# Weight-sum units, token sums, token loads and the gate row at other steps of a fused attention and SwiGLU block

## The chip, the cores and the metric

The kernel runs on one core of one Trainium2 chip. The metric is the device time of one execution in microseconds (us), a median over runs. Times inside an execution come from one profiled run of a kernel; they are counted from the first instruction.

The experiments ran in four batches on three chips, each batch with its own runs of the kernel before on the same chip.

## The reference, cut to what matters

```python
mod = silu(c) @ w_mod                      # six rows: sa, ca, ga, sb, cb, gb
h = layernorm(x) * (1 + ca) + sa           # x: 2048 tokens x 1024
q = h @ wq                                 # 32 heads of 128
o = softmax(q @ k.T / sqrt(128)) @ v       # the last 512 keys of 4 cached k/v heads
x = x + ga * (o @ wo)
h = layernorm(x) * (1 + cb) + sb
x = x + gb * ((silu(h @ w_gate) * (h @ w_up)) @ w_down)      # 3584 wide
```

## The kernel before

The tokens go through attention in two halves: attention 1, projection 1 (with `wo`), attention 2, projection 2. Then gate/up and the down projection follow, once per half. An attention is 64 steps; a step works on one head and 512 tokens. All large products but scores and values use a scheme with seven products instead of eight, which needs sums of weight blocks. These sums are made once, by GpSimd, as 58 **units**: 16 of `wo`, 28 of `w_gate` and `w_up`, 14 of `w_down`. A unit loads 512 KB into a staging slot of SBUF, does eight additions in place and writes 512 KB of sums to DRAM. Later loads fetch them.

A helper tracks which instruction last wrote or read a piece of SBUF and puts the waits in front of an instruction. All SBUF in question is one arena, where different tensors take the same bytes at different times. Each engine has a queue of its own, filled in the order in which the instructions are emitted. What stands behind a waiting instruction of ScalarE waits with it; the profile below shows this, with 21.77 us.

```python
OFF_ST = [131 * KB, 138 * KB]              # the two staging slots of units
OFF_U = 144 * KB                           # the slot in gate/up

def unit_step(ring):                       # emits one unit: load, sums, write
    k = un["c"]
    if k >= len(units):
        return
    while un["l"] - k < max(len(ring) - 1, 1):
        unit_ahead(ring)                   # load this one, if it is not loaded yet
    un["c"] += 1
    for n, _ in enumerate(unit_sums(k)):   # 4 pairs of additions on GpSimd
        if n == 1 and un["l"] - k < len(ring):
            unit_ahead(ring)               # with two slots: load the next one
    unit_write(k)

def unit_tick(i):                          # in an attention, NI = 64 steps
    if i % 5 in (0, 2):
        unit_step(OFF_ST if i % NI < NI - 14 else OFF_ST[1:])

def tick0(i):                              # attention 1; attention 2 likewise
    if i < 20 or i % 4 == 2:
        run_x()                            # a part of a gate row (ga or gb), if there is one
    wq_tick(0, i)
    if 6 <= i < NI - 8:
        unit_tick(i)

def o_units(sc, idx, j):                   # in a projection: 7 product groups
    if j == 1 and idx > 1 and (sc or idx % 2 == 0):
        unit_step(OFF_ST[1:])
```

The end of an attention also loads the weights of the projection. `start_o` names their places; the second part of the first set (131 KB on) and the second set (133 to 145 KB) lie over both staging slots:

```python
places = [[(OFF_WQ, 14), (131 * KB, 2)], [(133 * KB, 12), (OFF_E, 4)]] + ...

for i in range(lo, hi + 2):                # attend(): one step
    ...
    scores(i - 1)                          # TensorE, then exp on ScalarE
    pv(i - 2)                              # TensorE: needs that exp
    ...
    if i == hi - 6:
        start_o(sc)                        # first part of the first set
    if i == hi - 1:
        wo0[sc][0](0, (1,))                # these loads are issued by ScalarE
        wo0[sc][0](1)
```

`h_sums` makes four sums of token blocks on VectorE, each over 128 x 2048 elements, in a row. `stats_task` takes LayerNorm statistics of tokens in the background; its last two instructions per tile are on GpSimd.

The softmax here doesn't subtract the row's maximum and nothing guards it: scores larger than these inputs give would overflow.

## Time and profile before

| | before |
|---|---|
| median, range | 1223.62 us, 1223.05 to 1225.3 (4 runs) |
| span of the profiled run | 1223.2 us |
| TensorE busy | 1154.5 us, 94% |

Every product group needs the TensorE, so at 94% busy the kernel is bound by it, and what can still be won is its idle time, about 69 us. The page of the profile shows this; the first line gives busy times, the second a group of instructions (busy us and mean ns of one, then the idle time just before them and what ended most of it):

```profile
PE 1154.5 (94%) x7002; PEld 591.4 (48%) x7087; DVE 735.3 (60%) x1297; ACT 527.9 (43%) x735; POOL 452.8 (37%) x655
...
L273 PE MATMUL ps<-arena 128*128 128x512 f16 (+2 forms) x6697 | 1146.7, 332 | 64.5 <-ACT arena L784 31.0
```

The waits of the TensorE (total us, number, longest) blame the exponentials of line 784 first:

```profile
PE ps L273 <- ACT arena L784: 31.0, 5, 18.3
PE ps L273 <- DVE arena L806: 10.7, 2, 5.8
PE ps L273 <- issue: 4.1, 2, 3.9
```

The timeline of the end of attention 2 shows what stands behind this (start, duration, engine, line, operation; in brackets the idle time before it and its releaser). ACTq and POOL L950/L927 are DMA issues: L950 a unit's write, L927 a unit's load.

```profile
587.99 0.65 POOL L950 DMA_DIRECT2D wgu_sum<-arena  x1 [0.30 <-POOL arena L882]
...
589.53 0.80 POOL L927 DMA_DIRECT2D arena<-in_B_w_down_dram  x1
593.25 12.15 ACTq L1144 DMA_DIRECT2D arena<-in_A_wo_dram  x3
...
601.15 0.57 POOL L950 DMA_DIRECT2D wd_sum<-arena  x1 [0.30 <-POOL arena L943]
...
605.45 2.14 ACT L784 ACTIVATE arena<-ps 128x1024 bf16<-128x1024 f32 x2 [21.77 <-POOL rstd L419]
...
607.64 17.56 PE L273 MATMUL ps<-arena 128*128 128x129 bf16 x81 [18.34 <-ACT arena L784]
```

ScalarE stands still from 583.68 to 605.45, the 21.77 us in the bracket, with three loads in front of the exponentials in its queue. The line of 593.25 merges the three. Their places lie over the slots, so each waits until its slot is free. The exponentials start at 605.45, and the TensorE goes on at 607.64 after 18.34 us. The bracket of line 605.45 names an instruction of GpSimd that merely ran last before. The end of attention 1 looks the same, with 10.95 us (its line of 255.41 merges a load at 255.41 and two at 269.43):

```profile
255.41 15.25 ACTq L1144 DMA_DIRECT2D arena<-in_A_wo_dram  x3
...
266.40 0.57 POOL L950 DMA_DIRECT2D wgu_sum<-arena  x1 [0.30 <-POOL arena L882]
270.72 2.14 ACT L784 ACTIVATE arena<-ps 128x1024 bf16<-128x1024 f32 x2 [14.38 <-issue]
...
272.91 1.91 PE L273 MATMUL ps<-arena 128*128 128x129 bf16 x16 [10.95 <-ACT arena L784]
```

The windows (busy us and instructions of TensorE, weight loads, VectorE, ScalarE, GpSimd; then granted clock, DMA share, GB/s) show that a long wait costs more than itself. For 4 us after it the TensorE has half its clock:

```profile
607.60:611.70 4.10, 4.06 (x22) 2.62 (x23) 0.87 (x2) 0.00 (x0) 0.00 (x0) 0.50 0.98 319
611.70:616.00 4.30, 4.25 (x20) 1.89 (x20) 2.87 (x4) 0.00 (x0) 0.00 (x0) 0.99 0.15 30
```

Third, GpSimd's own timeline shows how the units run: the first in projection 1 (299.20), the first in attention 2 (373.81), and some in its middle:

```profile
299.20 0.94 POOL L927 DMA_DIRECT2D arena<-in_B_w_gate_dram  x1 [32.23 <-PE ps L273]
...
373.81 0.93 POOL L927 DMA_DIRECT2D arena<-in_B_w_up_dram  x1 [22.14 <-ACT tmp L817]
...
426.91 0.59 POOL L950 DMA_DIRECT2D wgu_sum<-arena  x1 [0.30 <-POOL arena L882]
...
433.79 0.94 POOL L927 DMA_DIRECT2D arena<-in_B_w_up_dram  x1 [3.05 <-DMA wgu_sum<-arena]
...
438.90 0.59 POOL L950 DMA_DIRECT2D wgu_sum<-arena  x1 [0.30 <-POOL arena L882]
```

These two writes are 12 us apart; over attention 2 it is (601.15 - 373.81) / 22 = 10.3 us per unit. The waits between them are for DMA transfers of the units themselves, never for another engine. New units are offered every 2.5 steps of 3.5 us, so every 8.75 us. GpSimd therefore falls behind all through attention 2.

Last, the four token sums of attention 1 delay what VectorE must do for the TensorE:

```profile
117.78 1.68 DVE L830 TENSOR_TENSOR arena<-arena 128x2048 f16<-128x2048 f16 x1
...
120.34 1.91 PE L273 MATMUL ps<-arena 128*128 128x129 bf16 x16 [4.96 <-DVE arena L806]
```

### The profile page before, as it was taken

To read this page: it belongs to the slowest core of one execution; us is meant where nothing else is said; L and a number is where in the kernel's file an instruction comes from. 1 tells how busy PE (TensorE), PEld (TensorE's weight loads), DVE (VectorE), ACT (ScalarE), POOL (GpSimd) and SP (SyncE) were. 2 spreads that over 40 slices of the span, in tenths; PEclk is the share of its full clock that TensorE was granted. 3 is DMA by queue.
4 is the path that set the end of the run, shared out by engine and by line. 5 is a ranking of instruction groups with operands and counts; after the bars stand their busy time and mean duration, and the time that the engine had idled before them with its cause. 6 is when DMAs were issued, how large, how long until landed. Compare 5 with 4: busy or idle time off the path is not lost.

```text
span 1223.2 us, 18300 instructions
## 1 busy us (share of the span) xinstructions
PE 1154.5 (94%) x7002; PEld 591.4 (48%) x7087; DVE 735.3 (60%) x1297; ACT 527.9 (43%) x735; POOL 452.8 (37%) x655
## 2 busy tenths in 40 slices
PE   8698999969999999999399899999999999999998
PEld 5465556634445556655244344444444444444443
DVE  4757866627695666677185856554575654454535
ACT  3465777730106777787101044545301245454110
POOL 1366887630525766687514434544000000000000
PEclk9999999989999999999699999999999999999999
DMA  9985999886856999988578577867667465554453
GB/s 329 207 189 145 212 201 223 183 197 176 241 155 134 203 200 201 196 205 205 161 189 227 191 254 230 270 203 250 206 181 226 137 190 185 169 175 140 136 176 108
DMA packets 305895, 238.72 MB, mean 195 GB/s; under 512 B 132240, under 2 KB 279696, under 8 KB 305808
## 3 DMA queue, kind: packets, MB, share of 16 engines
q1 hardware_dynamic: 234800, 121.67, 42.1%
q0 software_dynamic: 16704, 60.82, 16.3%
q10 hardware_dynamic: 54304, 55.05, 14.2%
q8 instruction: 56, 0.92, 0.3%
q14 instruction: 31, 0.25, 0.1%
HBM read 172.49 MB, written 34.60 MB: 169 GB/s over the span
## 4 chain that ended last, share of the span: by engine, by line
PE 60%; DMA 16%; POOL 15%; DVE 4%; issue 3%; ACT 1%; ACTq 0%; POOLq 0%; DVEq 0%; SPq 0%
PE ps L273 60%; POOL arena L882 8%; DMA wgu_sum<-arena 6%; POOL arena L943 4%; DMA arena<-in_B_w_gate_dram 4%; DMA wo_sum<-arena 2%; DMA arena<-in_B_w_up_dram 2%; POOL arena L927 2%; DMA arena<-nsc 1%; DVE arena L433 1%; ACT arena L784 1%; POOL rstd L421 0%; DMA arena<-in_B_w_down_dram 0%; DMA arena<-in_A_wo_dram 0%; DVE x_res L1108 0%
## 5 line engine op out<-in xcount | busy, mean ns | idle before, releaser
L273 PE MATMUL ps<-arena 128*128 128x512 f16 (+2 forms) x6697 | 1146.7, 332 | 64.5 <-ACT arena L784 31.0
L273 PEld LDWEIGHTS ps<-arena 128*128 128x128 bf16 (+1 forms) x6782 | 581.2, 99 | 623.2 <-ACT arena L784 33.4
L784 ACT ACTIVATE arena<-ps 128x1024 bf16<-128x1024 f32 x256 | 261.4, 1022 | 95.7 <-PE ps L273 47.7
L817 ACT ACTIVATE tmp<-ps 128x512 f32<-128x512 f32 x166 | 99.1, 597 | 307.9 <-PE ps L273 295.5
L943 POOL TENSOR_TENSOR arena<-arena 128x256 f16<-128x256 bf16 x240 | 176.3, 740 | 92.3 <-DMA arena<-in_B_w_down_dram 70.4
L882 POOL TENSOR_TENSOR arena<-arena 128x256 f16<-128x256 bf16 x224 | 166.4, 743 | 62.7 <-DMA arena<-in_B_w_gate_dram 28.9
L814 DVE TENSOR_TENSOR arena<-ps,tmp 128x512 bf16<-128x512 f32 (+1 forms) x134 | 91.9, 685 | 56.7 <-PE ps L273 52.6
L803 DVE RECIPROCAL rl<-ps 128x4 f32<-128x4 f32 x128 | 23.2, 181 | 142.6 <-PE ps L273 142.4
L814 DVE TENSOR_TENSOR arena<-ps,nsc 128x512 f16<-128x512 f32 x84 | 57.8, 688 | 80.4 <-PE ps L273 68.8
L817 ACT ACTIVATE nsc<-ps 128x512 f32<-128x512 f32 x84 | 50.1, 597 | 99.5 <-PE ps L273 97.1
L806 DVE TENSOR_TENSOR arena<-ps,rl 128x512 f16<-128x512 f32 x128 | 88.5, 691 | 4.4
L1039 DVE TENSOR_TENSOR arena<-arena 128x2048 f16<-128x2048 f16 (+3 forms) x56 | 57.9, 1044 | 13.5 <-PE ps L273 12.9
L1470 ACT ACTIVATE arena<-arena 128x512 f16<-128x512 f16 x84 | 49.8, 624 | 30.6 <-DVE arena L814 30.6
L882 DVE TENSOR_TENSOR arena<-arena 128x512 f16<-128x512 bf16 x104 | 56.2, 540 | 0.2
L814 DVE TENSOR_TENSOR tmp<-ps,tmp 128x512 f32<-128x512 f32 x32 | 22.1, 690 | 54.4 <-ACT tmp L817 45.5
L817 ACT ACTIVATE arena<-ps 128x512 f32<-128x512 f32 x16 | 9.6, 597 | 94.0 <-PE ps L273 91.2
L414 DVE BATCH_NORM_STATS2 st<-x_res 128x6 f32<-128x512 bf16 x62 | 42.2, 681 | 3.8 <-DMA x_res<-in_A_x_dram 3.4
L1487 DVE TENSOR_TENSOR arena<-ps,arena 128x512 f16<-128x512 f32 x28 | 19.4, 692 | 36.7 <-PE ps L273 36.7
L927 POOL DMA_DIRECT2D arena<-in_B_w_down_dram x14 | 11.0, 788 | 72.3 <-DMA wd_sum<-arena 44.6
L1485 DVE TENSOR_TENSOR arena<-arena 128x512 f16<-128x512 f16 x84 | 35.1, 442 | 0.3
L1107 DVE TENSOR_TENSOR tmp<-tmp,rowb 128x512 f32<-128x512 f32 x48 | 33.8, 704 | 1.6
L428 DVE TENSOR_SCALAR nsc<-x_res,mv,rstd 128x1024 f16<-128x1024 bf16 (+1 forms) x30 | 17.8, 594 | 26.8 <-DMA arena<-nsc 25.6
(85 smaller groups left out, 427.6 us busy)
## 6 DMA issues: line engine op xcount, KB each, us to landing
arena<-wgu_sum SPq DMA_DIRECT2D x56, 512.0 KB, 6.8
arena<-in_A_wq_dram SPq DMA_DIRECT2D x28, 512.0 KB, 5.5
wgu_sum<-arena POOLq DMA_DIRECT2D x28, 512.0 KB, 5.0
arena<-wo_sum ACTq DMA_DIRECT2D x7, 2048.0 KB, 9.8
arena<-in_B_w_gate_dram SPq DMA_DIRECT2D x28, 512.0 KB, 4.1
arena<-in_B_w_up_dram SPq DMA_DIRECT2D x28, 512.0 KB, 6.5
arena<-wd_sum ACTq DMA_DIRECT2D x8, 1792.0 KB, 7.9
arena<-in_B_w_down_dram ACTq DMA_DIRECT2D x6, 1792.0 KB, 7.2
```

What stands on the lines that cost most here:

```text
L273: T.op(PE, lambda: TE.matmul(out_ap, lhsT, rhs, start=start, stop=stop, skip_group_check=skip), reads=reads, writes=[bank_buf])
L414: T.op(DVE, lambda: V.bn_stats(st_[sl][:, hf * 6:hf * 6 + 6], x_res[:, t, hf * 512:hf * 512 + 512]), reads=[B_x[t]], writes=[B_st[sl]])
L784: T.op(ACT, lambda: A.activation(ex_s[es][:, 2 * kp:2 * kp + 2, :], banks2(SCB + 2 * kp), AF.Exp, scale=att_scale), writes=[PB[SCB + 2 * k ...
L806: T.op(DVE, lambda: V.tensor_tensor(o_s[os_].rearrange("p (a b) d -> p a b d", a=2), psap(PVB * 512, [[512, 2], [130, 2], [1, P]]), rlb, A ...
L814: T.op(DVE, lambda: V.tensor_tensor(out, bank(ba), other, ADD), reads=[ob2], writes=[PB[ba], ob])
L817: T.op(ACT, lambda: A.activation(dst, bank(bk), AF.Copy), writes=[PB[bk], db])
L882: T.op(st, lambda: eng.tensor_tensor(o[:, h * n:h * n + n, :], x, y, op), reads=rd, writes=[wr])
L927: T.op(Q_of[slot][0], lambda: g.dma_start(dst, src), writes=[w.b_raw, w.b_s3])
L943: T.op(POOL, lambda: g.tensor_tensor(o[:, c], a[:, c], b[:, c], SUB), reads=rd, writes=[wr])
L1039: T.op(DVE, lambda: V.tensor_tensor(o, a, b, SUB), reads=rd, writes=[sb])
L1470: T.op(ACT, lambda: A.activation(o, s_, AF.Silu), reads=[sb], writes=[ob])
L1485: T.op(DVE, lambda: V.tensor_tensor(gu[blk][:, p, :], o, s_, MULT), reads=[sb, ob], writes=[B_gu[blk][p]])
```

## The change

The intent of the change: units stop ahead of each attention's end, with both slots drained, so that the loads and exponentials find them free; units that are lost there are made elsewhere; the token sums go one per step; tokens are loaded and their statistics taken later in attention 1; the parts of the gate row go to another quarter of the steps. The core of the diff (cut: the places where the token sums are now advanced in the projections and the down projection, and where the sums of `wq` are):

```diff
                 T.op(DVE, lambda: V.tensor_tensor(tT[0], b12, b11, SUB), ...)
+                yield                       # and after each of the other three
...
-                if k >= len(units):
+                if k >= len(units) or not (ring or un["l"] > k):
                     return
-                while un["l"] - k < max(len(ring) - 1, 1):
+                while ring and un["l"] - k < max(len(ring) - 1, 1):
                     unit_ahead(ring)
...
-            LOADX = {6: 2, 12: 3}
+            LOADX = {14: 2, 20: 3}
...
-                    unit_step(OFF_ST if i % NI < NI - 14 else OFF_ST[1:])
+                    unit_step(OFF_ST if i % NI < NI - 12 else ())
...
-                if i == 21:
-                    h_sums()
-                if i == 14:
+                if i == 26:
                     bg.append(stats_task(2 * TPC, 2 * TPC))
             def tick0(i):
-                if i < 20 or i % 4 == 2:
+                if i < 20 or i % 4 == 0:
                     run_x()
+                if i == 21:
+                    hs[0] = h_sums()
+                if 21 <= i < 25:
+                    next(hs[0])
-                if 6 <= i < NI - 8:
+                if 10 <= i < NI - 8:
                     unit_tick(i)
...
-                if j == 1 and idx > 1 and (sc or idx % 2 == 0):
+                if j == 1 and idx > 1 and (sc == 0 or idx < 5):
                     unit_step(OFF_ST[1:])
...                                          # attention 2:
-                if i % 4 == 2:
+                if i % 4 == 0:
                     run_x()
...                                          # gate/up:
-                    if sc == 0 and r < FP - 3:
+                    if sc == 0:
                         unit_step([OFF_U])
```

Counted from the order of GpSimd's instructions, the units per stage go from 20, 3, 22, 5, 8 to 18, 5, 22, 3, 10 (attention 1, projection 1, attention 2, projection 2, gate/up).

More of the change, by code (lines that the diff above doesn't have):

```diff
@@ L827, in h_sums @@
                 T.op(DVE, lambda: V.tensor_tensor(tT[0], b12, b11, SUB), reads=B_hT[0][0:HK] + B_hT[1][0:HK], writes=B_T[0])
+                yield
                 T.op(DVE, lambda: V.tensor_tensor(tT[1], b22, tT[0], SUB), reads=B_hT[1][HK:DT] + B_T[0], writes=B_T[1])
+                yield
                 T.op(DVE, lambda: V.tensor_tensor(b12, b22, b12, SUB), reads=B_hT[1][HK:DT], writes=B_hT[1][0:HK])
+                yield
                 T.op(DVE, lambda: V.tensor_tensor(tT[2], b21, tT[1], SUB), reads=B_hT[0][HK:DT] + B_T[1], writes=B_T[2])
+                yield
             def rhs(n):
@@ L1250, in pre0 @@
                     take_oT(3)
-                if i == 21:
-                    h_sums()
                 mods(i)
-                if i == 14:
+                if i == 26:
                     bg.append(stats_task(2 * TPC, 2 * TPC))
             wo0 = {}
+            hs = [None]
             def tick0(i):
-                if i < 20 or i % 4 == 2:
+                if i < 20 or i % 4 == 0:
                     run_x()
+                if i == 21:
+                    hs[0] = h_sums()
+                if 21 <= i < 25:
+                    next(hs[0])
                 wq_tick(0, i)
-                if 6 <= i < NI - 8:
+                if 10 <= i < NI - 8:
                     unit_tick(i)
@@ L1332, in o_units @@
             def o_units(sc, idx, j):
-                if j == 1 and idx > 1 and (sc or idx % 2 == 0):
+                if j == 1 and idx > 1 and (sc == 0 or idx < 5):
                     unit_step(OFF_ST[1:])
+            sums2 = []
             def o_hook0(idx, j):
@@ L1341, in o_hook0 @@
                     take_wq(1, 1)
-                if idx == 5 and j == 1:
-                    wq_of[1, 0].sums(DVE, V)
+                if idx == 5 and j < 2:
+                    if j == 0:
+                        sums2.append(wq_of[1, 0].sum_ops(DVE, V))
+                        sums2.append(wq_of[1, 1].sum_ops(DVE, V))
+                    next(sums2[0])
+                    next(sums2[0])
                 if idx == 5 and j == TPC - 1:
@@ L1346, in o_hook0 @@
                         run_bg(1)
-                    h_sums()
-                    wq_of[1, 1].sums(DVE, V)
+                    hs[0] = h_sums()
+                    next(hs[0])
+                if idx == 6:
+                    if j < 3:
+                        next(hs[0])
+                    if j > 0:
+                        next(sums2[1], None)
+                        next(sums2[1], None)
                 if idx == 6 and j == 2:
@@ L1416, in o_hook1 @@
                         run_bg(1)
-                    h_sums()
+                    hs[0] = h_sums()
+                    next(hs[0])
+                if idx == 6 and j < 3:
+                    next(hs[0])
             while bg:
@@ L1592, in f_hook @@
                     run_bg(1)
-                    if sc == 0 and idx == 6 and j == 1:
-                        while bg:
-                            run_bg(1)
-                        h_sums()
+                    if sc == 0 and idx == 6:
+                        if j == 0:
+                            while bg:
+                                run_bg(1)
+                            hs[0] = h_sums()
+                        next(hs[0])
                 seven_products(FP, gu, B_gu, OFF_GU, m1, ver, (0, 1, 2, 3), (4, 5, 6, 7), f_out(sc, sc == 1), sj, False, f_hook)
```

## The prediction

> **What bounds the kernel now.** The busy table has the TensorE at 1154.5 of 1223.2 us (94%): 69 us idle. Windows of 20 us place it: the start (0-60, 13 us); 113-120 (5); 260-273 (11); 360-380 (2.8); 554-570 (2.5); 589-608 (18.3); 689-693 (3.9). The two largest are the ends of the two attentions. The wait table blames the exponentials (31 us in 5 waits); the timeline shows why they are late: ScalarE's in-order queue sits in three loads of the output weights (255.4, 15.3 us; 593.3, 12.2 us). Their space is the two staging slots of GpSimd's weight-sum units, so they go out only when the last unit's write has landed (issued 601.15, loads released at about 605.4). After the stall the TensorE runs at a granted clock of 0.50 for 4 us (607.6-611.7), some 2 us more. The Trainium skill, "TensorE: Matmul & The Clock Gate", Part 1, says that some 3.4 us of idleness halve the clock; this trace agrees.
>
> **What changes.** No work is added or removed. The order of GpSimd's instructions gives weight-sum units per stage (attention 1, projection 1, attention 2, projection 2, gate/up): before 20, 3, 22, 5, 8; after 18, 5, 22, 3, 10.
>
> *Attention 1.* GpSimd no longer waits for token statistics early (11.9 us at 97-110), two units go, and the last no longer take 17-18 us each in one slot. Its last write should land near 230, before the loads (241, 255). The stall of 11 us and 2 us of half clock go: -13. The token sums, spread over four steps, save about 4.5 of the 5 us at 113-120. Projection 1 starts about 18 us earlier.
>
> *Attention 2.* Here I do not expect the intended gain. In 382-580 GpSimd is paced by its own chain (load about 6 us, eight sums of 0.74, write about 5): 10.2 us per unit, while units are offered every 2.5 steps of 3.5 us = 8.75 us. It never waits for TensorE there and ends 40 us behind, so the end of the stall is the end of this chain. After the change the chain starts in projection 1 about 18 us earlier (load at 299.2 becomes 281), but has five units there in one slot. Projection 2 shows five such units taking 84 us (633.8-717.9). So attention 2's first load comes at about 366, against 373.8: 7 us earlier. Loading the last unit ahead saves some 3 us. ScalarE is released about 10 us earlier, though TensorE arrives over 20 us earlier: this stall grows from 18 to about 30 us and swallows the savings at 113-120, 360-380 and of the gate row (2 x 1.2 us).
>
> *After that.* The wait of 3.9 us at 689 is a weight load on saturated DMA (about 350 GB/s); its neighbours are unchanged, so it stays. In gate/up ten units of 16.8 us end at about 886 on the present clock; the loads that need them go out at 891.7: at most 0-4 us lost.
>
> **Sum:** 1223 - 10 - 1 for smaller gains: **1212 us**, 8 in 10 within 1202 to 1219. Faster by over 2%: 0.10; within 2%: 0.88; slower: 0.02.
>
> **What would show it.** Right: no wait at the end of attention 1; GpSimd's writes in attention 2 still 10 us apart, the last near 590; a TensorE wait of 25-35 us there. Wrong: that wait under 10 us (then about 1185), or a new wait at the down projection's third product group.
>
> **What would make it wrong.** GpSimd faster than 10 us a unit in attention 2; five units in projection 1 taking 70 or 100 us; the earlier unit loads delaying attention 1.

## The result and the profile after

| | before | after |
|---|---|---|
| median, range | 1223.62 us, 1223.05 to 1225.3 (4 runs) | 1209.83 us, 1208.31 to 1216.0 (4 runs) |
| ratio | 1 | 0.9895 (95%: 0.9859 to 0.993) |
| span of the profiled run | 1223.2 us | 1207.6 us |
| wait at the end of attention 1 | 10.95 us | 0.51 us |
| wait at the end of attention 2 | 18.34 us | 27.67 us |

A ratio is the mean time of one kernel's fast runs over that of the other's of the same rounds, so it is not quite the ratio of the medians in the table. The gain of about 1% is clear of the noise, as the interval excludes 1. A run counts as slow here when it is over 1.5% above the fastest of its kernel.

On the page of the kernel after, the TensorE's busy time is nearly the same; the idle time before its products has fallen by 13.3 us, less than the two ends of the attentions and the token sums had promised:

```profile
PE 1151.8 (95%) x7087; PEld 587.9 (49%) x7087; DVE 742.4 (61%) x1297; ACT 527.4 (44%) x735; POOL 456.2 (38%) x655
...
L273 PE MATMUL ps<-arena 128*128 128x512 f16 (+2 forms) x6782 | 1144.7, 331 | 51.2 <-ACT arena L784 29.2
```

Its waits: the exponentials are still first, and now they are almost all one wait:

```profile
PE ps L273 <- ACT arena L784: 29.2, 4, 27.7
...
PE ps L273 <- DVE arena L806: 5.9, 2, 5.4
...
PE ps L273 <- issue: 2.8, 1, 2.8
```

The timeline of the end of attention 1 (after): ScalarE's three loads go in 2.23 us, the exponentials follow at 251.37, and the TensorE runs from 247.23 on without a break:

```profile
247.23 37.94 PE L273 MATMUL ps<-arena 128*128 128x512 bf16 x210 [0.51 <-ACT arena L784]
...
248.29 2.23 ACTq L1148 DMA_DIRECT2D arena<-in_A_wo_dram  x3
...
251.37 2.14 ACT L784 ACTIVATE arena<-ps 128x1024 bf16<-128x1024 f32 x2 [2.17 <-PE ps L273]
```

The timeline of the end of attention 2 (after). It is the same picture as before, with the last unit written from 588.59 and the exponentials at 592.96:

```profile
581.04 0.58 POOL L954 DMA_DIRECT2D wgu_sum<-arena  x1 [0.30 <-POOL arena L886]
...
584.09 8.82 ACTq L1148 DMA_DIRECT2D arena<-in_A_wo_dram  x3
588.59 0.65 POOL L954 DMA_DIRECT2D wd_sum<-arena  x1 [0.30 <-POOL arena L947]
...
592.96 2.14 ACT L784 ACTIVATE arena<-ps 128x1024 bf16<-128x1024 f32 x2 [32.34 <-POOL rstd L419]
...
595.16 17.11 PE L273 MATMUL ps<-arena 128*128 128x129 bf16 x82 [27.67 <-ACT arena L784]
```

The TensorE arrived here at 595.16 - 27.67 = 567.5, against 607.64 - 18.34 = 589.3 before: 21.8 us earlier. It left 12.5 us earlier. The other 9.3 us were given back in this wait. GpSimd's timeline (after) tells why:

```profile
278.82 0.92 POOL L931 DMA_DIRECT2D arena<-in_B_w_gate_dram  x1 [45.61 <-PE ps L273]
...
366.08 0.57 POOL L954 DMA_DIRECT2D wgu_sum<-arena  x1 [0.30 <-POOL arena L886]
366.71 0.93 POOL L931 DMA_DIRECT2D arena<-in_B_w_up_dram  x1
...
424.80 0.58 POOL L954 DMA_DIRECT2D wgu_sum<-arena  x1 [0.30 <-POOL arena L886]
...
436.17 0.59 POOL L954 DMA_DIRECT2D wgu_sum<-arena  x1 [0.30 <-POOL arena L886]
```

The chain of units starts at 278.82, 20.4 us earlier than before. It makes five units in projection 1, until 366.08, and starts attention 2's at 366.71, only 7.1 us earlier than before. Then it goes at its pace of (588.59 - 366.71) / 22 = 10.1 us per unit. The gain from 10.3 to 10.1 is all in the last unit, which is now loaded ahead: from the write before to its own write pass 7.6 us (581.04 to 588.59), against 13.2 before (587.99 to 601.15). The other 21 units take 10.2 us each in both kernels.

In all ten fast profiles that have such a wait with ScalarE's loads in front of the exponentials (before, after and the variants below), the TensorE goes on 6.5 to 6.6 us after the last unit's write is issued, wherever that write lies between 574.53 and 601.15.

In the stretch of the token sums (98 to 145 us) the TensorE's wait for VectorE has fallen from 4.96 to 1.5 us:

```profile
PE ps L273 <- DVE arena L814: 1.5, 1, 1.5
```

### The profile page after: what moved, and what is told of

It reads as the page before. It is cut to its first block, busy times and chain, and to the rows that moved or that the text cites. A ratio compares the mean times of both kernels' runs of the same rounds, so it can differ in the third digit from the quotient of the medians.

```text
span 1207.6 us, 18388 instructions
## 1 busy us (share of the span) xinstructions
PE 1151.8 (95%) x7087; PEld 587.9 (49%) x7087; DVE 742.4 (61%) x1297; ACT 527.4 (44%) x735; POOL 456.2 (38%) x655
## 4 chain that ended last, share of the span: by engine, by line
PE 69%; DMA 14%; POOL 11%; DVE 3%; issue 3%; ACT 1%; ACTq 0%; POOLq 0%; DVEq 0%; SPq 0%
PE ps L273 69%; POOL arena L886 9%; DMA wgu_sum<-arena 7%; DMA arena<-in_B_w_up_dram 3%; DMA arena<-in_B_w_gate_dram 3%; POOL arena L931 1%; DMA arena<-nsc 1%; POOL arena L947 0%; DVE st L414 0%; ACT arena L784 0%; DVE arena L814 0%; POOL rstd L421 0%; DVE arena L806 0%; DVE arena L433 0%; DVE arena L678 0%
## 5 line engine op out<-in xcount | busy, mean ns | idle before, releaser
L886 DVE TENSOR_TENSOR arena<-arena 128x512 f16<-128x512 bf16 x104 | 58.9, 567 | 1.7 <-DMA arena<-in_A_wq_dram 1.5
L931 POOL DMA_DIRECT2D arena<-in_B_w_gate_dram x14 | 13.1, 936 | 67.7 <-PE ps L273 45.6
```

The lines of the kernel that those rows point to most:

```text
L886: T.op(st, lambda: eng.tensor_tensor(o[:, h * n:h * n + n, :], x, y, op), reads=rd, writes=[wr])
L931: T.op(Q_of[slot][0], lambda: g.dma_start(dst, src), writes=[w.b_raw, w.b_s3])
```

## The experiments

In their texts "chain theory" is the reading above: what ends the wait at the end of attention 2 is the last unit's write, and that lies as many unit times after the chain's start as there are units. GpSimd's time is the budget, not the TensorE's. Unless said otherwise, the times of units are read from each run's profile, and each edit is against one of the two kernels. All results were correct.

### Units alone, and all but the units

The first has only the unit parts of the diff above, on the kernel before:

```diff
+ unit_step, unit_tick, 10 <= i in tick0, o_units and gate/up as in the change
```

> The kernel before with only the new schedule of the weight-sum units (18, 5, 22, 3, 10 per stage); token sums, token loads, statistics and gate row as before. Chain theory (the end of attention 2 is the end of GpSimd's chain of units, and its start is the start of projection 1's second product group): the 13 us at the end of attention 1 go, the chain starts 13 us earlier, but two more units in projection 1 cost it about 20 us more than the 22 us in which it idled there; ScalarE is released only 5 to 7 us earlier. About 1217 us (-6), wait at the end of attention 2 about 26 us. Rival (the intent as stated: stopping the units early is what pays, the rest is trimming): nearly all of the 14 us, 1210 to 1212 us.

Measured: 1218.92 us median (1217.84 to 1221.32, 4 runs), ratio 0.9977 (0.9921 to 1.0034). In the profile the wait at the end of attention 1 is gone (0.5 us) and that at the end of attention 2 is 25.0 us. The last unit is written from 595.43.

The second is the changed kernel with those parts undone:

```diff
- unit_step, unit_tick, 10 <= i in tick0, o_units and gate/up as in the change
+ as before
```

> The changed kernel with the old schedule of the units (20, 3, 22, 5, 8). Chain theory: later statistics and spread sums free GpSimd and VectorE in attention 1, so its stall at the end falls from 11 to about 5 us, projection 1 starts about 13 us earlier, and with three units there the chain of attention 2 starts as soon as its slot is free, some 15 us earlier than before: about 1209 us, as fast as the whole change. Rival: 1217 us or more, since the long stalls at the attention ends are untouched.

Measured: 1212.67 us median, but 1202.85 and 1203.75 in two runs and 1221.6 and 1221.69 in two others, which count as slow; ratio of the fast ones 0.9847 (0.976 to 0.9934). The profiled run is one of the slow ones, so I take nothing from it. The mean of all four over the mean of all seven runs of before is 0.991.

What follows: the units alone gained at most 0.8%, as the chain theory said (the rival's 1210 to 1212 us, a ratio of about 0.99, lies outside the interval). An 11 us wait that comes before another wait was removed, with two more units placed between them, and the time hardly moved. How much the rest gains alone is not settled by two and two runs; the two slow ones lie less than 1 us above the limit for slow.

### Fewer units ahead of attention 2's end

Two variants of the changed kernel attack the chain. One makes three units in projection 1 and five in projection 2, as before the change, the other makes five in both and 20 in attention 2:

```diff
 # first                                                       (18, 3, 22, 5, 10)
-                if j == 1 and idx > 1 and (sc == 0 or idx < 5):
+                if j == 1 and idx > 1 and (sc or idx % 2 == 0):
 # second                                                      (18, 5, 20, 5, 10)
-                if j == 1 and idx > 1 and (sc == 0 or idx < 5):
+                if j == 1 and idx > 1:
-                    unit_step(OFF_ST if i % NI < NI - 12 else ())
+                    unit_step(OFF_ST if i % NI < NI - (12 if i < NI else 17) else ())
```

> The changed kernel, but with the units of the projections as before: three in projection 1, five in projection 2 (18, 3, 22, 5, 10). Chain theory: attention 2's first unit load comes at about 354 instead of 367, its last write 12 us earlier, the wait at its end falls from 27.7 to about 15 us: about 1197 us. Rival (that wait is set by something else than when the chain starts): no change, 1210 us.

Measured: 1205.06 us median (1195.2 to 1212.17, 4 runs), ratio 0.9856 (0.9774 to 0.9937). Attention 2's first load comes at 353.29, its last write at 574.53, and the wait is 15.5 us, as expected. But the time is 8 us above the 1197 expected: the profile has a new wait of 6.8 us in gate/up, for a load of `w_up`.

> The changed kernel, but attention 2 gets 20 units instead of 22, and projection 2 five instead of three (18, 5, 20, 5, 10). Chain theory: two units of 10.1 us less in the chain, the wait at the end of attention 2 falls from 27.7 to about 8 us: about 1190 us, up to 3 us more if the ten units of gate/up now end too late for the down projection. Rival: the same 1210 us.

Measured: 1203.8 us median (1199.18 to 1213.15, 4 runs), ratio 0.9868 (0.9779 to 0.9957). The wait fell to 15.3 us, not to 8: attention 2's chain started at 367.96 as expected, but its units took (575.57 - 367.96) / 20 = 10.4 us each. The time is 14 us above the 1190 expected: besides the 7 us of the wait, the TensorE left attention 2 13.0 us earlier than in the profile of the changed kernel, but the span is only 7.1 us shorter, and where the other 6 us went was not traced. Both of these runs refute the rival that the wait is set by something else. With the waits, the size was right to 0.5 us in the first and off by 7 in the second. That the total is shorter than the changed kernel's is not shown by these two runs: both intervals contain its 0.9895.

### The changed kernel again, and ScalarE's order

On another chip, with five rounds: the changed kernel unaltered, and one with two lines moved, so that in attention 2 the loads stand behind the last exponentials in ScalarE's queue.

```diff
-                    if i == hi - 1:
+                    if i == hi - (1 if sc == 0 else 0):
                         wo0[sc][0](0, (1,))
                         wo0[sc][0](1)
```

> The changed kernel unaltered, as a control on this chip: 0.985 to 0.99 of before, with a wait of 25 to 31 us at the end of attention 2 that ends when the last unit's write has landed.

Measured: 1214.41 us median (1204.67 to 1216.16, 6 runs), ratio 0.993 (0.9888 to 0.9972), above the stated 0.985 to 0.99. The wait was 34.9 us long, over the stated 25 to 31, and it ended as expected, after the last unit's write:

```profile
593.65 0.65 POOL L954 DMA_DIRECT2D wd_sum<-arena  x1 [0.30 <-POOL arena L947]
...
600.21 4.47 PE L273 MATMUL ps<-arena 128*128 128x129 bf16 x22 [34.90 <-ACT arena L784]
```

The chain shows what was larger: the five units of projection 1 took 93.0 us here (277.02 to 369.98), against 87.3 in the first profile, and attention 2's first load came at 370.60. Why they took longer is not known.

> The changed kernel, but at the end of attention 2 ScalarE issues the two loads that wait for the staging slots one step later, behind the last exponentials. Chain theory (the slots are the cost, not the order of ScalarE's queue): the exponentials and the last products of attention run some 25 us earlier, but the output projection then waits for its weights until the same chain has ended; total within 2 us of the changed kernel, the wait moved to a DMA load. Rival (the wait table's own reading, that the exponentials are the cost): the wait vanishes, 25 us gained, about 1185 us.

Measured: 1204.6 us median (1197.19 to 1208.25, 6 runs), ratio 0.9863 (0.9823 to 0.9902). Its timeline:

```profile
562.25 2.14 ACT L784 ACTIVATE arena<-ps 128x1024 bf16<-128x1024 f32 x2 [2.58 <-PE ps L273]
...
587.74 0.58 POOL L954 DMA_DIRECT2D wgu_sum<-arena  x1 [0.30 <-POOL arena L886]
...
590.78 9.05 ACTq L1148 DMA_DIRECT2D arena<-in_A_wo_dram  x3
...
593.61 10.76 PE L273 MATMUL ps<-arena 128*128 128x512 bf16 x36 [25.27 <-DMA arena<-in_A_wo_dram]
...
595.29 0.65 POOL L954 DMA_DIRECT2D wd_sum<-arena  x1 [0.30 <-POOL arena L947]
...
605.82 19.37 PE L273 MATMUL ps<-arena 128*128 128x512 bf16 x87 [1.46 <-DMA arena<-in_A_wo_dram]
```

The exponentials now start at 562.25, the wait is one for a load, and it is still 25.27 us long (34.9 in the unaltered kernel of the same batch). The 25 us that the wait table seemed to offer are not there: the slots are the cost. But the gain, 8 us on the means of the same rounds (1212.4 and 1204.2), is four times the 2 us that I had allowed. The timeline shows two reasons. The last products of attention are done before the wait. And the TensorE goes on at 593.61, before the last unit is even written (595.29): it first needs the load into the first slot, which the unit before the last had left (written from 587.74). In the old order the exponentials had stood behind all three loads, and so behind the last unit. Counted from that unit's write, the TensorE goes on 1.7 us before it here and 6.6 us after it in the unaltered kernel; that is the 8 us.

### The two other parts by themselves

```diff
 # on the kernel before: token sums of attention 1, one per step
-                if i == 21:
-                    h_sums()
+                hs[0] = h_sums() at i == 21 in tick0, next(hs[0]) at 21 <= i < 25
```

> The kernel before with only the four token sums of attention 1 spread over four steps. The wait of 5 us near 113-120 falls to about 1 us, so projection 1's chain of units starts about 4 us earlier. But attention 1's end is itself held by GpSimd's last unit there, which does not move: the wait at the end of attention 1 grows by the same 4 us. Total within 2 us of before. Rival (the saved VectorE time counts directly): 4 to 5 us faster.

Measured: 1224.94 us median (1215.12 to 1237.96, 4 runs, the last of them slow), ratio 1.0014 (0.9936 to 1.0091). No gain can be seen, within an interval of nearly 1% to both sides. In the profile the longest wait near the sums fell to 2.7 us, but the wait at the end of attention 1, expected to grow by 4 us, was 11.1 us and so hardly grew, and the last unit there was written at 264.87 instead of 266.40. The total agrees with the chain theory, its detail was not seen, and the interval does not exclude 4 us.

```diff
 # on the kernel before
-            LOADX = {6: 2, 12: 3}
+            LOADX = {14: 2, 20: 3}
-                if i == 14:
+                if i == 26:
                     bg.append(stats_task(2 * TPC, 2 * TPC))
```

> The kernel before with only the later token loads (steps 14 and 20) and the later statistics of tokens (step 26). GpSimd no longer waits for them around 100, so attention 1's last unit should be written some 7 us earlier than 266. The 5 us of token sums stay, so TensorE comes no earlier to the end of attention 1, but its wait there shrinks by the same 7 us; projection 1's chain, attention 2's chain and the end of its wait all move with it: about 1216 us, ratio 0.993 to 0.995. Together with the token sums alone (no gain) this would make up the gain of everything but the units. Rival (only TensorE's own waits count, and this touches none): no change.

Measured: 1223.48 us median (1216.65 to 1229.39, 6 runs), ratio 1.0026 (0.9977 to 1.0075). This is a miss: 7 us were expected and the interval allows at most 3, so the rival's "no change" fits better. The wait at the end of attention 1, expected to shrink, was 10.8 us. The profiled run had its last unit of attention 1 written at 261.15 instead of 266.40 and was 5.6 us shorter than the profiled run of before, which however is from another session. The timed runs of the same rounds do not bear this out. So the split of the whole gain among the parts stays open. The gate row's move, and the sums in the projections and the down projection, were not run by themselves at all.

### The new wait in gate/up

The first variant with three units in projection 1 once more, and the same with a slot of its own for projection 2's units. That slot lies over keys and values, which are dead by then, and not over the third pair of gate/up weights (128 to 144 KB):

```diff
-            Q_of = {... for o in OFF_ST + [OFF_U]}
+            Q_of = {... for o in OFF_ST + [OFF_U, 145 * KB]}
-                if j == 1 and idx > 1 and (sc == 0 or idx < 5):
-                    unit_step(OFF_ST[1:])
+                if j == 1 and idx > 1 and (sc or idx % 2 == 0):
+                    unit_step([145 * KB] if sc else OFF_ST[1:])
```

> The first variant with three units in projection 1 and five in projection 2 again, on another chip, as a partner for the next run. It showed a new TensorE wait of 6.8 us in gate/up: the fifth unit of projection 2 sits in a slot that the third gate/up weight pair is loaded over, and that load blocks the queue behind it. Expected: the wait of about 15 us at the end of attention 2 again, and 0 to 7 us for that load; 1200 us give or take 5.

Measured: 1208.97 us median (1196.9 to 1214.85, 6 runs), ratio 0.9878 (0.983 to 0.9927). This is above the stated 1195 to 1205. By the record the chip was the one of the first batch, not another. The wait at the end of attention 2 was 18.7 us, where about 15 were expected. Its timeline in gate/up (SPq L1426 is a load of gate/up weights):

```profile
709.71 0.57 POOL L954 DMA_DIRECT2D wd_sum<-arena  x1 [0.30 <-POOL arena L947]
...
712.72 0.37 SPq L1426 DMA_DIRECT2D arena<-in_B_w_up_dram  x1
...
716.97 3.26 PE L273 MATMUL ps<-arena 128*128 128x512 f16 x8 [6.45 <-DMA arena<-in_B_w_up_dram]
```

The fifth unit of projection 2 is written from 709.71; at 712.72 the load over its slot can go; 4.2 us later the TensorE, which has waited 6.45 us for it, goes on.

> The same unit counts (18, 3, 22, 5, 10), but projection 2's units in a slot that no weight pair is loaded over and that is free when attention 2 ends. If the slot is the cause of the new wait, it vanishes, and the units of projection 2 start some 25 us earlier: up to 7 us faster than the partner. If only the count of units (their traffic) is the cause, no change.

Measured: 1198.98 us median (1191.53 to 1208.97, 6 runs), ratio 0.9806 (0.9753 to 0.9859). In the same stretch (650 to 720 us) no wait for a load is left. The longest is the one that before has too:

```profile
PE ps L273 <- issue: 4.6, 1, 4.6
```

On the means of the same rounds that is 8.0 us (1207.0 and 1199.0), with the counts of units the same. The six runs of each scatter so much that this difference has a standard error of about 4 us; the two profiled spans differ by 7.7 us, of which the vanished wait is 6.45. So that wait comes from the slot and not from the count of units. With their own slot these units also start earlier (587.29 instead of 612.20), and the run does not part the two. In the changed kernel the part `idx < 5` avoids the wait in another way: its three units there are written by 672.01. The kernel before has five there in the same slot and shows no wait for a load between 650 and 790 us.

### A version made from the theory

The chain theory says what to do: give attention 2 as many units as GpSimd can make until the TensorE gets there, and put the rest where GpSimd has time. Attention 1 takes 20, its statistics coming later still; attention 2 takes 19; projection 2 takes six, in a slot of its own.

```diff
 # on the changed kernel                                       (20, 3, 19, 6, 10)
-                    unit_step(OFF_ST if i % NI < NI - 12 else ())
+                    unit_step(OFF_ST if i % NI < NI - (9 if i < NI else 18) else ())
-                if 10 <= i < NI - 8:
+                if 6 <= i < NI - 8:
-                if i == 26:
+                if i == 40:
                     bg.append(stats_task(2 * TPC, 2 * TPC))
-                if j == 1 and idx > 1 and (sc == 0 or idx < 5):
-                    unit_step(OFF_ST[1:])
+                if j == 1 and (idx > 1 and idx % 2 == 0 if sc == 0 else idx > 0):
+                    unit_step([145 * KB] if sc else OFF_ST[1:])
```

> A version made from the theory: units 20, 3, 19, 6, 10. Attention 1 takes two more (its statistics later, at step 40, so GpSimd does not wait for them early), attention 2 three fewer, projection 2 six in a slot of their own that needs no wait for a weight buffer and blocks none. Chain theory: attention 2's chain starts at about 354 and ends at about 550 to 560, when TensorE arrives; the wait there falls from 28 to under 6 us: about 1182 us (1178 to 1192). Rival: no better than 1205.

Measured: 1184.69 us median (1177.6 to 1186.48, 6 runs), ratio 0.9695 (0.9658 to 0.9732). On the means of the same rounds (1183.7 against 1212.4 of the changed kernel) it is 2.4% faster than the change. Several things differ at once here, so this tests the theory as a whole and no part of it alone. In its timeline the loads take 1.84 us, and the TensorE runs on through the end of attention 2:

```profile
556.65 31.82 PE L273 MATMUL ps<-arena 128*128 128x512 bf16 x178 [0.51 <-ACT arena L784]
557.70 1.84 ACTq L1148 DMA_DIRECT2D arena<-in_A_wo_dram  x3
...
560.79 2.14 ACT L784 ACTIVATE arena<-ps 128x1024 bf16<-128x1024 f32 x2 [2.16 <-PE ps L273]
```

Its largest wait is now another, in the down projection, for sums that gate/up's ten units finish too late:

```profile
PE ps L273 <- DMA arena<-wd_sum: 8.2, 1, 8.2
...
PE ps L273 <- ACT arena L784: 1.7, 3, 0.7
```

One more turn of the same screw:

```diff
 # on the version above                                        (20, 3, 20, 6, 9)
   attention 2 ends one unit later, gate/up makes one unit fewer,
   and ScalarE's two loads stand behind the last exponentials
```

> Units 20, 3, 20, 6, 9, in the slots of the version made from the theory (which ran at 1184.7 and still waited 8.2 us for the last sums in the down projection), and the two loads at the end of attention 2 one step later. One unit fewer in gate/up ends that chain about 17 us earlier, so the 8.2 us go; attention 2's chain ends about 10 us later, at about 560, which the later loads should hide up to 3 us. About 1177 us (1173 to 1184).

Measured: 1183.54 us median (1176.52 to 1189.36, 6 runs), ratio 0.969 (0.9652 to 0.9729), on another chip than the version above (0.9695), so no difference can be claimed. The wait of 8.2 us is gone, as expected; in the profile waits of 4.9 us (at the end of projection 2), 3.3 and 1.3 us stand in its place. The expected 7 us did not come, and 1183.54 is just inside the stated 1173 to 1184.

## Why the prediction was right

- **Size.** 1212 was predicted, 1209.83 measured; in the repeat on another chip 1214.41. Both lie in the stated range of 1202 to 1219.
- **Attention 1.** The stall and its half clock go: right (0.51 us left). The prediction put the start of projection 1's chain 18 us earlier; it was 20.4. That the units leave early enough (last write near 230) was right too: 232.6.
- **Projection 1.** Five units in one slot were to take 84 us, read from projection 2 of the kernel before; they took 366.08 - 278.82 = 87.3. Attention 2's first load was predicted at 366 and came at 366.7. That it fits this well is partly luck: the chain started 2.2 us earlier than the predicted 281, and its five units took 3.3 us longer. In the repeat they took 93.0 us.
- **Attention 2.** A chain at 10.2 us per unit, the last write near 590, a wait of 25 to 35 us: measured 10.1, 588.6 and 27.7. ScalarE was to be released 10 us earlier; it was 605.45 - 592.96 = 12.5. The term that was too small is the last unit loaded ahead: about 3 us were allowed, and it saved 13.2 - 7.6 = 5.6. This step carried the prediction. A look at the two waits alone would have promised their sum, 29 us. The variants with fewer units ahead of the end of that wait shortened it each time (15.3 to 18.7 us), and the version made from the theory removed it.
- **Token sums, gate row.** They were to save TensorE time that the later wait swallows. The wait near the sums fell by 3.5 us (4.5 predicted), and the 9.3 us given back at the end of attention 2 show the swallowing for the sum of all savings. For the single parts it is not shown: their timed runs could not tell 0 from 3 or 4 us.
- **Later stages.** Gate/up's last unit is written from 866.1 and the first load that needs it goes out at 876.8, so nothing was lost, as predicted. The wait of 3.9 us at the end of projection 2 was to stay; it was 2.8. Together with the 12.5 us this gives 13.6 of the 15.6 us between the two profiled spans; the rest I have not traced.

The wait table's first line was misleading in the way the prediction said. The run with the loads behind the exponentials showed it, and also corrected me: the order of ScalarE's queue is worth 8 us, not under 2, because it decides whether the TensorE waits for the last unit or only for the one before.

## What to carry to other kernels

A wait ends when the slowest chain that feeds it ends, so before you cost a saving ahead of it, find that chain, its start and its pace, and count its links; time saved on the other side of the wait only makes the wait longer. When a compute instruction is blamed for a wait, look at what stands in front of it in its own engine's queue: a DMA issue that waits for a buffer held everything behind it here. A buffer shared between a background job and a critical load is a schedule constraint of its own; moving the job's work elsewhere, with another buffer for a part of it, gained 28.7 us here over the changed kernel (1212.4 and 1183.7), and the reordering of ScalarE's queue 8.2 us. The other buffer alone gained 8.0 us, no more than the reordering.

## What the Trainium skill lacked or had wrong

- Not wrong, but to be read with care: "TensorE: Matmul & The Clock Gate", Part 1, says that after an idle window of about 3.4 us the clock is halved, and that about 3.4 us of work bring it back. The trace of before agrees in size: the granted clock is 0.50 from 607.6 to 611.7, which is 4.1 us, after a wait of 18.3 us. But the half clock was only 2 us of a loss of 20 us here; the rest was the wait itself.
- The same page, "Architectural detail", says that ScalarE's queue is strictly first in, first out. The trace agrees: after the change, ScalarE had been idle for 32.34 us when the last exponentials came, while DMA issues stood in front. What is lacking: I found no page with the advice that follows, namely that a DMA issue with an unmet wait should not stand in front of work that the TensorE needs. Moving it back by one step changed the mean from 1212.4 to 1204.2 us.
- "Perfetto Trace Analysis", section "Per-instruction lifecycle", says that waits on semaphores fall outside the reported window, so that an instruction can look fast where the kernel is slow. The trace agrees: in narrow windows the first of ScalarE's three loads at the end of attention 2 (before) has a record of 0.38 us at 593.25, and the other two one of 1.23 us together at 604.17. The stretch of 12.15 us shown above is the view's merging of the three, with a wait between them. The wait table charged the TensorE's 18.3 us to the exponentials behind them, so the cause has to be looked for in the gap.
- I found no page that gives a pace for a background chain of a load, additions on GpSimd and a write through one or two slots. The runs show 9.9 to 10.4 us per unit of 512 KB with two slots (attention 2 of all profiles), and 16.8 to 19.5 us with one (84.1 / 5 in projection 2 before, 87.3 / 5 in projection 1 after, 97.5 / 5 in projection 2 of the repeated variant).
- I found no page that warns how far runs of one single-core kernel lie apart. In the batches of experiments the kernel before took between 1210.7 and 1238.6 us.
